# One list of token numbers in DRAM instead of two, written through two disjoint views

## The chip, the cores and the metric

The kernel runs on one core of one Trainium2 chip. The metric is the time of one execution on the device, in microseconds (us); the time of a kernel is the median of its timed runs. A profile is taken of one execution more. Five engines work side by side, each with its own queue of instructions: TensorE (PE, with its weight loads as PEld), VectorE (DVE), ScalarE (ACT), GpSimd (POOL) and SyncE (SP). They wait for each other, and for DMA transfers, through semaphores. A transfer whose rows are chosen by a list of indices (an indirect DMA) is issued from POOL's queue here, all others from SP's.

## What is computed

Three stages follow each other on 4608 tokens of width 512: chunked attention (chunks of 64), a dense layer with squared ReLU (512 to 2048 to 512), and a layer of 8 experts of which each token takes one, chosen by the largest logit.

```python
# x: [4608, 512], the output of attention
h = x @ w_in; r = np.maximum(h, 0.0); x = (s * (r * r) + b) @ w_out
logits = x @ w_gate + modality_bias[modality_id]
e_idx = np.argmax(logits, axis=1)
gate_w = softmax(logits)[arange(N), e_idx]
for e in range(E):
    mask = e_idx == e
    h = np.maximum(x[mask] @ w1[e], 0.0)
    out[mask] = gate_w[mask, None] * (h @ w2[e])
```

## The kernel before, in words

**Blocks.** The tokens are cut into 18 blocks of 256, two tiles of 128 each. For each block the dense layer runs as 16 steps f: `m_l1(j, f)` makes 128 of the 2048 hidden columns (L413), squares them on ACT and splits them into a high and a low part; the low part, gl, is a subtraction on POOL (L428). `m_l2` (L486) uses gh and gl two steps later. Attention of the next block and the routing of the block before run between these steps. The order of the instructions on every engine is the order of the program: the whole kernel is traced under a manual schedule.

**Routing.** For block j the kernel finds the expert of each token, the rank of the token among all tokens of that expert so far (`g_rank`, L635 and L636, matmuls against a triangle), and from both the place `e * 4608 + rank` (`g_dest`). `g_scatter(j)` (L658) then writes the numbers of the tokens to their places in a list in DRAM, one indirect DMA for each of the two tiles (L661). There are two lists, `ids[0]` for the first tile of every block and `ids[1]` for the second. Both are filled with 2^19 at the start (L1231); a token's number is written as number - 2^19. The sum of the two lists at a place is thus the token's number where one of the tiles wrote it, and 2^20 where none did. The rows of the tokens, scaled, go to `ys` in DRAM.

**Units.** The expert layer runs over units of 128 places in the list. `u_ids(u, idx)` (L808) gathers the 128 numbers of a unit, from both lists into two columns; `u_gather(u)` adds the columns on POOL (L816) and gathers the 128 rows of `ys` with the sum as index into `xg` (L818), where indices past the end fetch nothing. `u_x(u)` transposes xg on PE (L952) and splits it into two halves of 16 bits; `u_l1` (L973, L977) and `u_l2` (L999) are the two matmuls; the result is scattered to the rows of `out` with the same index (L1006).

**The seam between the two.** The first four units (0 to 3, "lead") belong to the expert that has most tokens after block 15; their places are filled by then, so their numbers and rows are fetched during the last block's steps. All later units need the last block's routing: `routing()` runs g_scatter(17), then `u_tables`, which works out each unit's expert and places (`gidx`, L908), then `ids_to(1)` (the numbers of units 4 and 5), `fetch` of unit 4's rows and then the numbers of unit 6. After that each unit fetches the numbers of a unit some four further on and the rows of the one three further on. PE's order is fixed: the transposes of unit 4's rows stand ahead of the second half of unit 3's first matmul.

An access to DRAM waits for earlier accesses to the same tensor that it depends on: a number gather for the landing of the scatters into its list, a scatter for the landing of the scatter before into the same list.

Of the kernel before, what the change touches and what calls it, by code (L numbers as in the profile page):

```python
# [7 lines left out]

F32 = mybir.dt.float32
# [3 lines left out]
I32 = mybir.dt.int32  # L13
U32 = mybir.dt.uint32
AF = mybir.ActivationFunctionType
ALU = mybir.AluOpType
# [2 lines left out]
DRAM = bass.MemoryType.DRAM  # L19
EXP_MASK = 0x7F800000  # L20


HALF = 1 << 19


def pow2(n):
# [4 lines left out]
def kernel(  # L31
# [16 lines left out]
    nc = tc.nc  # L48
    P = 128
    B, H, S, HD = q.shape  # L50
    NT, DM = out.shape
    FF = w_in.shape[1]
    E, _, F2 = w1.shape
# [4 lines left out]
    NTB = TB // P  # L58
    NB = NT // TB
    NTILE = NT // P  # L60
# [14 lines left out]
    def pool(name, bufs=1, side="left", st=None):  # L75
# [5 lines left out]
    dram = ctx.enter_context(tc.tile_pool(name="dram", bufs=1, space=DRAM))  # L81
# [6 lines left out]

    ys = dram.tile([NT, ROW], F32, name="ys")

    ids = [dram.tile([E * NT + P, 1], I32, name=f"ids{t}") for t in range(NTB)]
    wgt = dram.tile([E, DM], F32, name="wgt")
    wd = [
        dram.tile([E * P, 4096 + (TAIL if i == 0 else 0)], F16, name=f"wd{i}") for i in range(4)
# [9 lines left out]
        out=tri, in_=ones, pattern=[[1, P]], compare_op=ALU.is_gt, fill=0.0,  # L104
        base=0, channel_multiplier=-1,
# [3 lines left out]
    def iota(name, shape, pattern, base=0, cm=0):  # L109
        ti = tmp.tile(shape, I32, tag="i", name=name + "_i")  # L110
        nc.gpsimd.iota(ti, pattern=pattern, base=base, channel_multiplier=cm)
        tf = const.tile(shape, F32, name=name)
        nc.vector.tensor_copy(tf, ti)
        return tf
# [1 line left out]
    rev8 = iota("rev8", [P, NTB, E], [[0, NTB], [-1, E]], base=E)  # L116
    ebase = iota("ebase", [P, NTB, E], [[0, NTB], [NT, E]])
    tokid = const.tile([P, NTILE], I32, name="tokid")
    nc.gpsimd.iota(tokid, pattern=[[P, NTILE]], base=-HALF, channel_multiplier=1)
    eidx = iota("eidx", [P, E], [[1, E]])  # L120
    slot = iota("slot", [P, NRP], [[0, NRP]], cm=1)
    uidx = iota("uidx", [P, NRP], [[1, NRP]])
# [35 lines left out]
    def small(n, shape, dt=F32, bufs=None):  # L158
        return sm.tile(shape, dt, tag=n, name=n, **({"bufs": bufs} if bufs else {}))
# [498 lines left out]
    def g_scatter(j):  # L658
        di = rank.pop(j)
        for t in range(NTB):  # L660
            nc.gpsimd.indirect_dma_start(  # L661
                out=ids[t], out_offset=bass.IndirectOffsetOnAxis(ap=di[:, t, :], axis=0),
                in_=tokid[:, j * NTB + t:j * NTB + t + 1], in_offset=None,
            )

# [102 lines left out]
    uid = {}  # L768
# [34 lines left out]
        nc.sync.dma_start(out=dst, in_=wd[i][bass.ds(e * P, P), cols], **kw)  # L803

    def u_ids(u, idx):
        two = uid[u] = small("uid2", [P, NTB], I32, 6)
        for t in range(NTB):
            nc.gpsimd.indirect_dma_start(  # L808
                out=two[:, t:t + 1], out_offset=None, in_=ids[t],
                in_offset=bass.IndirectOffsetOnAxis(ap=idx, axis=0),  # L810
            )

    def u_gather(u):
        two = uid[u]
        uid[u] = small("uid", [P, 1], I32, 10)
        nc.gpsimd.tensor_tensor(out=uid[u], in0=two[:, 0:1], in1=two[:, 1:2], op=ALU.add)  # L816
        n = KNOWN_ROWS if u < NE else NT
        nc.gpsimd.indirect_dma_start(  # L818
            out=xg_t[u % 3], out_offset=None, in_=ys[:n],
            in_offset=bass.IndirectOffsetOnAxis(ap=uid[u], axis=0),  # L820
            bounds_check=n - 1, oob_is_err=False,
        )
# [284 lines left out]
    with tc.manual_schedule(engines=ENG):  # L1107
# [2 lines left out]
        nc.vector.memset(one_f, 1.0)  # L1110
        nc.vector.tensor_copy(one, one_f)
        none = su.tile([P, E * NTILE + 1], I32, tag="misc", name="none")
        nc.vector.memset(none, HALF)
        a_load(0)
        a_load(1)
        c_load(0)
# [66 lines left out]
        for s in range(2, NF + LEAD + LAG):  # L1183
# [43 lines left out]
                a_load(4)  # L1227
            if s == 7:
                nc.sync.dma_start(out=wg4, in_=w_gate.rearrange("(c p) e -> p c e", p=P))
                for t in range(NTB):  # L1230
                    nc.sync.dma_start(out=ids[t].rearrange("(p n) a -> p (n a)", p=P), in_=none)  # L1231
            if s == 8:
                v_load(4)
            if s == 9:
# [19 lines left out]
            if s == 17:  # L1254
# [6 lines left out]
                    out=wgb, in_=wgt.rearrange("e d -> (e d)").partition_broadcast(P)  # L1261
# [9 lines left out]
    with tc.manual_schedule(engines=ENG):  # L1271
# [46 lines left out]
        for f in range(NF):  # L1318
# [30 lines left out]
            if f == SCATTER:  # L1349
                g_scatter(j - 1)  # L1350
            if f in (4, 6, 8, 10):
                n = f // 2 - 2
                u_ids(n, early["gi"][:, n:n + 1])
            if f in (7, 9, 11):
                u_gather((f - 7) // 2)
# [131 lines left out]
```

## Time and profile before

| | us |
|---|---|
| timed runs, three | 1437.5, 1443.72, 1445.77 |
| their median | 1443.72 |
| the profiled execution's own time | 1438.02 |
| its span in the trace | 1436.3 |
| PE busy in the span | 1394.2 (97%) |
| DVE, ACT, POOL busy | 1070.7, 724.1, 435.7 |

The span goes from the first to the last instruction that the trace shows; 1.7 us lie around it. Busy times are of one engine each and overlap. [...]

### The profile page before, as it was taken

How to read it: one execution, taken by the hardware profiler on the slowest of the kernel's cores; microseconds unless marked ns; L12 is line 12 of the kernel's file. 1: busy time of each engine (PE TensorE's matmuls, PEld its weight loads, DVE VectorE, ACT ScalarE, POOL GpSimd, SP SyncE). 2: the span in 40 equal slices, each digit the busy share in tenths (PEclk: the TensorE clock that was granted, in tenths of full speed). 3: DMA queues.
4: the chain of work that ended last, by engine and by line, in shares of the span. 5: the costliest groups of instructions: out<-in, count | busy, mean ns of one | idle time of the engine just before them, and what ended most of it. 6: DMA issues, size and time to landing. Idle time of an engine off the chain costs nothing. (4 is left out here: it accounts for less than half of the span.)

```text
span 1436.3 us, 32039 instructions
## 1 busy us (share of the span) xinstructions
PE 1394.2 (97%) x11853; PEld 1151.0 (80%) x11853; DVE 1070.7 (75%) x2643; ACT 724.1 (50%) x1658; POOL 435.7 (30%) x515
## 2 busy tenths in 40 slices
PE   6899999999999999999999999998999999999995
PEld 5787888888888888888888888886767766776773
DVE  6987688877977977887697787767676676677662
ACT  4975555656565656655656565543233323333331
POOL 0000232332323333223323223463533433443320
PEclk9999999999999999999999999999999999999998
DMA  8673355555446443534534443461211231535340
GB/s 202 182 200 111 82 131 157 130 149 159 131 126 176 117 131 111 157 98 125 148 111 118 126 133 111 105 215 31 64 53 45 105 106 39 194 122 182 129 151 18
DMA packets 183886, 178.86 MB, mean 125 GB/s; under 512 B 131108, under 2 KB 139556, under 8 KB 179504
## 3 DMA queue, kind: packets, MB, share of 16 engines
q1 hardware_dynamic: 173392, 157.82, 37.7%
q0 software_dynamic: 10336, 18.97, 4.3%
q8 instruction: 95, 1.56, 0.5%
q14 instruction: 63, 0.52, 0.1%
HBM read 263.85 MB, written 54.14 MB: 221 GB/s over the span
## 5 line engine op out<-in xcount | busy, mean ns | idle before, releaser
L428 POOL TENSOR_TENSOR gl<-g,gh 128x256 fp32r<-128x256 f32 x256 | 221.6, 867 | 680.7 <-ACT gh L426 395.8
L413 PE MATMUL ph<-x,wi 128*128 128x256 f32 x2592 | 348.2, 285 | 5.0 <-ACT wi L232 3.8
L413 PEld LDWEIGHTS ph<-x,wi 128*128 128x128 f32 x2592 | 331.1, 190 | 20.2 <-ACT wi L232 4.4
L486 PE MATMUL py<-wo,gh 128*128 128x512 f32 x864 | 271.5, 395 | 0.2 <-DVE wo L166 0.2
L985 ACT ACTIVATE hr<-hr,scu 128x128 f32<-128x128 f32 x328 | 114.3, 396 | 282.0 <-DVE hr L166 262.4
L544 DVE CUSTOM_DVE_ANT_0 dump<-rows,wgb 128x512 bf16<-128x512 f32 x256 | 198.5, 775 | 5.0
L999 PEld LDWEIGHTS <-hh 128*128 128x128 f16 x984 | 95.0, 98 | 108.5 <-issue 2.2
L486 PE MATMUL py<-wo,gl 128*128 128x512 f32 x432 | 170.4, 395 | 0.0
L423 ACT ACTIVATE g<-ph 128x256 f32<-128x256 f32 x256 | 97.4, 380 | 136.1 <-PE ph L413 129.1
L486 PEld LDWEIGHTS py<-wo,gh 128*128 128x128 f32 x864 | 148.1, 188 | 21.8 <-DVE wo L166 0.5
L722 DVE SCALAR_TENSOR_TENSOR hl<-raw,wup,hl 128x512 f16<-128x512 f32 x128 | 111.1, 908 | 31.5 <-ACT hl L715 31.5
L973 PE MATMUL pu<-xhl,wa 128*128 128x256 f16 x736 | 127.9, 275 | 0.0
L977 PE MATMUL pu<-xhl,wa 128*128 128x128 f16 x736 | 125.4, 220 | 0.0
L999 PE MATMUL po<-wa,hh 128*128 128x512 f16 x552 | 124.6, 383 | 0.0
L715 ACT ACTIVATE hl<-raw,wup 128x512 f16<-128x512 f32 x128 | 85.5, 715 | 71.6 <-DVE wup L163 49.3
L413 PE MATMUL ph<-x,wj 128*128 128x256 f32 x864 | 116.7, 285 | 1.8 <-DVE wj L166 1.8
L981 DVE COPY hr<-pu 128x256 f32<-128x256 f32 x164 | 68.9, 420 | 61.5 <-PE pu L977 46.6
L1006 POOL DMA_INDIRECT out_dram<-o,uid x41 | 42.8, 1044 | 235.7 <-ACT o L1005 217.0
L413 PEld LDWEIGHTS ph<-x,wj 128*128 128x128 f32 x864 | 108.7, 189 | 6.3 <-DVE wj L166 2.0
L424 ACT ACTIVATE g<-g 128x256 f32<-128x256 f32 x256 | 107.5, 420 | 8.1
L426 ACT ACTIVATE gh<-g 128x256 fp32r<-128x256 f32 x256 | 107.4, 419 | 8.1
L973 PE MATMUL pu<-xhl,wb 128*128 128x256 f16 x576 | 98.9, 273 | 0.0
(216 smaller groups left out, 2271.9 us busy)
## 6 DMA issues: line engine op xcount, KB each, us to landing
wa<-wd SPq DMA_DIRECT2D x64, 1024.0 KB
wb<-wd SPq DMA_DIRECT2D x60, 1024.0 KB
raw<-in_moe_w_dram SPq DMA_DIRECT2D x64, 512.0 KB
wd<-hl SPq DMA_DIRECT2D x128, 256.0 KB
wb<-wd SPq DMA_DIRECT2D x20, 1030.5 KB
wa<-wd SPq DMA_DIRECT2D x20, 1030.5 KB
ys<-rows SPq DMA_DIRECT2D x18, 513.0 KB
vs<-in_v_dram SPq DMA_DIRECT2D x136, 64.0 KB
```

What stands on the lines that cost most here:

```text
L413: nc.tensor.matmul(ps, lhsT=wi_f(a, f)[:, kc], rhs=xt[j][b][:, kc, :], start=(n == 0), stop=(n == 3 * KC - 1),)
L423: nc.scalar.activation(out=g, in_=ps, func=AF.Relu)
L424: nc.scalar.activation(out=g, in_=g, func=AF.Square)
L426: nc.scalar.activation(out=hi, in_=g, func=AF.Copy)
L428: nc.gpsimd.tensor_tensor(out=lo, in0=g, in1=hi.bitcast(F32), op=ALU.subtract)
L486: nc.tensor.matmul(yps[j][t], lhsT=g[a][:, t * P:(t + 1) * P], rhs=wo_f(b, f), start=(f == 0 and n == 0), stop=(f == NF - 1 and n == 2),)
L544: nc.vector.tensor_tensor_reduce(out=dump, in0=ysb[j][:, t, :DM], in1=wgb[:, e * DM:(e + 1) * DM], scale=1.0, scalar=0.0, op0=ALU.mult, op ...
L722: nc.vector.scalar_tensor_tensor(out=hl[:, 1], in0=raw[:, a], scalar=sc, in1=hl[:, 0], op0=ALU.mult, op1=ALU.subtract)
L973: nc.tensor.matmul(ps[:, f], lhsT=w[:, kc, 0, cols], rhs=hl[:, :, kc, :], start=(kc == 0), stop=False,)
L977: nc.tensor.matmul(ps[:, f, 0], lhsT=w[:, kc, 1, cols], rhs=hl[:, 0, kc, :], start=False, stop=(kc == KC - 1),)
L985: nc.scalar.activation(out=r[:, f, :], in_=r[:, f, :], func=AF.Relu, scale=scu[:, c:c + 1])
L999: nc.tensor.matmul(ps, lhsT=hh[:, a, c, :], rhs=w[:, c % 4, b, :], start=(n == 0), stop=(n == 3 * NC2 - 1),)
```

## The change

The two lists become one. Both tiles of a block still scatter with one indirect DMA each, but into the same list, each through a view of its own; the views are declared disjoint, so that an access through the one isn't ordered against one through the other, while a read of the whole list is ordered behind both. Token numbers are written as they are, and an empty place holds 2^20. A unit gathers its numbers once, straight into the tile that serves as index; the add is gone. The initial fill is one store.

```diff
@@ -4,6 +4,7 @@
 import concourse.tile as tile
 from concourse import mybir
 from concourse._compat import with_exitstack
+from concourse.ap import dram_disjoint_views
 from concourse.masks import make_identity
 
 F32 = mybir.dt.float32
@@ -19,8 +20,7 @@
 DRAM = bass.MemoryType.DRAM
 EXP_MASK = 0x7F800000
 
-
-HALF = 1 << 19
+NONE = 1 << 20
 
 
 def pow2(n):
@@ -88,7 +88,8 @@
 
     ys = dram.tile([NT, ROW], F32, name="ys")
 
-    ids = [dram.tile([E * NT + P, 1], I32, name=f"ids{t}") for t in range(NTB)]
+    ids = dram.tile([E * NT + P, 1], I32, name="ids")
+    ids_v = dram_disjoint_views(ids, NTB)
     wgt = dram.tile([E, DM], F32, name="wgt")
     wd = [
         dram.tile([E * P, 4096 + (TAIL if i == 0 else 0)], F16, name=f"wd{i}") for i in range(4)
@@ -116,7 +117,7 @@
     rev8 = iota("rev8", [P, NTB, E], [[0, NTB], [-1, E]], base=E)
     ebase = iota("ebase", [P, NTB, E], [[0, NTB], [NT, E]])
     tokid = const.tile([P, NTILE], I32, name="tokid")
-    nc.gpsimd.iota(tokid, pattern=[[P, NTILE]], base=-HALF, channel_multiplier=1)
+    nc.gpsimd.iota(tokid, pattern=[[P, NTILE]], base=0, channel_multiplier=1)
     eidx = iota("eidx", [P, E], [[1, E]])
     slot = iota("slot", [P, NRP], [[0, NRP]], cm=1)
     uidx = iota("uidx", [P, NRP], [[1, NRP]])
@@ -659,7 +660,7 @@
         di = rank.pop(j)
         for t in range(NTB):
             nc.gpsimd.indirect_dma_start(
-                out=ids[t], out_offset=bass.IndirectOffsetOnAxis(ap=di[:, t, :], axis=0),
+                out=ids_v[t], out_offset=bass.IndirectOffsetOnAxis(ap=di[:, t, :], axis=0),
                 in_=tokid[:, j * NTB + t:j * NTB + t + 1], in_offset=None,
             )
 
@@ -803,17 +804,13 @@
         nc.sync.dma_start(out=dst, in_=wd[i][bass.ds(e * P, P), cols], **kw)
 
     def u_ids(u, idx):
-        two = uid[u] = small("uid2", [P, NTB], I32, 6)
-        for t in range(NTB):
-            nc.gpsimd.indirect_dma_start(
-                out=two[:, t:t + 1], out_offset=None, in_=ids[t],
-                in_offset=bass.IndirectOffsetOnAxis(ap=idx, axis=0),
-            )
+        uid[u] = small("uid", [P, 1], I32, 10)
+        nc.gpsimd.indirect_dma_start(
+            out=uid[u], out_offset=None, in_=ids,
+            in_offset=bass.IndirectOffsetOnAxis(ap=idx, axis=0),
+        )
 
     def u_gather(u):
-        two = uid[u]
-        uid[u] = small("uid", [P, 1], I32, 10)
-        nc.gpsimd.tensor_tensor(out=uid[u], in0=two[:, 0:1], in1=two[:, 1:2], op=ALU.add)
         n = KNOWN_ROWS if u < NE else NT
         nc.gpsimd.indirect_dma_start(
             out=xg_t[u % 3], out_offset=None, in_=ys[:n],
@@ -1110,7 +1107,7 @@
         nc.vector.memset(one_f, 1.0)
         nc.vector.tensor_copy(one, one_f)
         none = su.tile([P, E * NTILE + 1], I32, tag="misc", name="none")
-        nc.vector.memset(none, HALF)
+        nc.vector.memset(none, NONE)
         a_load(0)
         a_load(1)
         c_load(0)
@@ -1227,8 +1224,7 @@
                 a_load(4)
             if s == 7:
                 nc.sync.dma_start(out=wg4, in_=w_gate.rearrange("(c p) e -> p c e", p=P))
-                for t in range(NTB):
-                    nc.sync.dma_start(out=ids[t].rearrange("(p n) a -> p (n a)", p=P), in_=none)
+                nc.sync.dma_start(out=ids.rearrange("(p n) a -> p (n a)", p=P), in_=none)
             if s == 8:
                 v_load(4)
             if s == 9:
```

## Rows read from the trace of the kernel before

**Rows 1.** The page, busy time, share of the span and instructions of each engine

```profile
PE 1394.2 (97%) x11853; PEld 1151.0 (80%) x11853; DVE 1070.7 (75%) x2643; ACT 724.1 (50%) x1658; POOL 435.7 (30%) x515
```

**Rows 2.** Busy time by stage; columns: stretch, length, each engine's busy time, clock, DMA share

```profile
160.00:926.00 766.00, 763.61 (x6615) 675.76 (x6614) 606.94 (x1581) 455.23 (x1043) 240.36 (x274) 1.00 0.47 129
...
985.00:1010.00 25.00, 22.55 (x181) 15.96 (x179) 19.78 (x57) 6.50 (x18) 14.05 (x15) 0.93 0.20 63
1010.00:1385.00 375.00, 375.00 (x3158) 264.14 (x3157) 256.74 (x580) 119.20 (x309) 143.74 (x171) 1.00 0.32 108
```

**Rows 3.** Waits of PE from 900 us on: who waited for whom, total, times, longest

```profile
PE px L952 <- DMA xg<-ys,uid: 2.5, 1, 2.5
PE prk L636 <- DVE oh L166: 2.3, 1, 2.3
```

**Rows 4.** Timeline of POOL and DVE, 984 to 1001 us: start, length, engine, line, what

```profile
984.64 1.01 POOL L661 DMA_INDIRECT ids<-tokid,di  x1 [19.58 <-DVE cnt L861]
...
985.96 0.97 POOL L661 DMA_INDIRECT ids<-tokid,di  x1 [0.30 <-issue]
...
990.51 0.20 DVE L908 SCALAR_TENSOR_TENSOR gidx<-row,slot 128x40 int32<-128x40 f32 x1
...
994.04 1.10 POOL L808 DMA_INDIRECT uid<-ids,gidx  x1 [7.11 <-DMA ids<-tokid,di]
...
995.45 1.07 POOL L808 DMA_INDIRECT uid<-ids,gidx  x1 [0.30 <-issue]
...
998.25 0.95 POOL L808 DMA_INDIRECT uid<-ids,gidx  x1 [0.30 <-issue]
...
999.22 0.20 POOL L816 TENSOR_TENSOR uid<-uid 128x1 int32<-128x1 int32 x1
...
999.69 1.11 POOL L818 DMA_INDIRECT xg<-ys,uid  x1 [0.27 <-issue]
```

**Rows 5.** Timeline of PE, 1003 to 1016 us

```profile
1003.19 0.66 PE L952 MATMUL px<-ident,xg 128*128 128x128 f32 x4 [2.45 <-DMA xg<-ys,uid]
1003.68 0.27 PE L973 MATMUL pu<-xhl,wa 128*128 128x256 f16 x1
...
1007.98 5.34 PE L999 MATMUL po<-wa,hh 128*128 128x512 f16 x24
...
1013.16 0.27 PE L973 MATMUL pu<-xhl,wa 128*128 128x256 f16 x1
...
1015.80 0.39 PE L952 MATMUL px<-ident,xg 128*128 128x128 f32 x2
```

**Rows 6.** Half microseconds without and with DMA packets, columns as in rows 2

```profile
988.00:988.50 0.50, 0.50 (x9) 0.47 (x7) 0.47 (x2) 0.00 (x0) 0.00 (x0) 1.00 0.00 0
...
996.00:996.50 0.50, 0.50 (x4) 0.26 (x3) 0.47 (x2) 0.00 (x0) 0.50 (x1) 1.00 0.04 1
```

**Rows 7.** Clock after two idles of PE, columns as in rows 2, and the earlier one's wait

```profile
1005.00:1007.00 2.00, 2.00 (x15) 1.53 (x13) 1.90 (x5) 0.00 (x0) 1.32 (x1) 0.50 0.34 131
...
116.00:118.00 2.00, 2.00 (x20) 2.00 (x19) 1.93 (x5) 1.97 (x4) 0.00 (x0) 1.00 0.05 12
...
PE ph L413 <- DVE wj L166: 1.8, 1, 1.8
```

**Rows 8.** POOL's groups of instructions with count, busy, mean ns; and one wait, 1010 to 1385 us

```profile
L808 POOL DMA_INDIRECT uid<-ids,gidx x74 | 71.6, 968 | 29.4 <-issue 21.3 <-DMA ids<-tokid,di 7.1 <-DVE hr L166 0.9
...
L816 POOL TENSOR_TENSOR uid<-uid 128x1 int32<-128x1 int32 x41 | 9.4, 229 | 0.9
...
POOL out_dram L1006 <- ACT o L1005: 179.4, 32, 5.8
```

**Rows 9.** Timeline of POOL and PE behind an earlier block's scatters, 864 to 873 us

```profile
864.20 0.98 POOL L661 DMA_INDIRECT ids<-tokid,di  x1 [0.15 <-issue]
...
866.98 0.73 POOL L428 TENSOR_TENSOR gl<-g,gh 128x256 fp32r<-128x256 f32 x1 [0.51 <-issue]
...
872.18 0.40 PE L486 MATMUL py<-wo,gl 128*128 128x512 f32 x1
```

## The prediction

> **What bounds the kernel now.** I read the page first. TensorE (PE) is busy for 1394.2 of the 1436.3 us of the span, GpSimd (POOL) for 435.7 [rows 1]. A change that takes work off POOL can therefore only pay where PE waits for POOL, so the next view is the busy time by stage. From 160 to 926 us PE is busy 763.61 of 766.00 us, and from 1010 to 1385 us, where the experts' units run, 375.00 of 375.00; only the 25 us from 985 to 1010 stand out in the part that the change touches, with 22.55 busy and a granted clock of 0.93 [rows 2]. The waits of PE say what it lacked there: from 900 us to the end the list has three, and one of them ends in something that the change touches: the transposes of line 952 waited 2.5 us for the rows that unit 4 gathers (xg). The 2.3 us of the ranking matmul are DVE's and stay; the third is 0.2 us [rows 3].
>
> The timeline of POOL and DVE shows what makes unit 4's rows late. Unit 4 is the first whose tokens are known only after the last block was routed. POOL issues the last block's two scatters at 984.64 and 985.96. The indices for the number gathers are ready when DVE ends gidx at 990.51 + 0.20 = 990.71, but the first number gather starts at 994.04, after 7.11 us of idle that the scatter ended. Then come four number gathers (two lists, units 4 and 5), the last from 998.25 to 999.20, the add at 999.22 and the row gather at 999.69, which takes 1.11 us [rows 4]. PE resumes at 1003.19, that is 2.39 us after the issue of the row gather ended [rows 4, 5]. Everything in that chain is in one file on POOL, and PE has nothing else to do.
>
> **The change part by part, on the path.** (1) After the change the first number gather reads the one list, so it waits for both tiles' scatters instead of the first's alone. Call the delay d. It isn't above 995.45 - 994.04 = 1.41 us, because the gather from the second list started at 995.45 behind an idle of just 0.30 us on issue and so found its scatter landed; it isn't below 0 unless one list makes the scatters land sooner, for which no row speaks. The two scatters are issued 985.96 - 984.64 = 1.32 us apart [rows 4]; I take half of that, d = 0.7, since the second one had the same time or less to land and nothing shows when in those 1.41 us it did. (2) One gather for unit 4 (1.10 us) and one for unit 5 (1.07 us, with 0.30 us of issue before it) remain of the four [rows 4]: the first ends at 994.04 + 0.7 + 1.10 = 995.84, the second at 995.84 + 0.30 + 1.07 = 997.21, and POOL is free for the row gather near 997.5. (3) The add is gone, and with it the cover: the row gather itself now waits for unit 4's numbers to land. The nearest row for that is the DMA share: the gather whose issue ended at 995.14 shows its packets between 996.0 and 996.5, so within 1.4 us of the end of its issue [rows 4, 6]. That lands the numbers near 995.84 + 1.4 = 997.2; with 0.5 us to notice it, as an estimate between the 0.30 of an issue that waits for nothing and a little more, the row gather starts at 997.7 instead of 999.69: 2.0 us sooner. The bounds: at best d = 0 and the row gather goes as soon as POOL is free, 994.04 + 1.10 + 0.30 + 1.07 + 0.30 = 996.8, which is 2.9 us sooner and closes the whole 2.45 us; at worst d = 1.41 and the numbers need the 2.7 us from 996.52 (end of unit 4's second number gather) to 999.22 (the add that didn't have to wait): 994.04 + 1.41 + 1.10 + 2.7 + 0.3 = 999.55, 0.1 us sooner. Behind the waiting row gather stand unit 6's numbers and the output scatter of a finished unit; nothing on PE waits for either within 10 us. So PE's wait falls from 2.45 to about 0.45 us: **2.0 us**, between 0.1 and 2.45.
>
> (4) The wait costs twice. After it the granted clock is at the lower of its two levels, 0.50 from 1005 to 1007 [rows 7], and the 32 matmuls of the half unit that begins at 1003.68 last until 1007.98, 4.30 us, while the same half unit takes from 1013.16 to 1015.80, 2.64 us, at the full clock [rows 5]: 1.66 us. An idle of 1.8 us, near 115 us, left the clock at 1.00 [rows 7]. If 0.45 us remain (or anything under 1.8, that is, if the row gather comes 0.65 us sooner or more), I expect no fall: another **1.66 us**.
>
> What is late next? The rows of unit 5 are needed at 1015.80 [rows 5], their chain moves forward with unit 4's, and from 1010 on PE has no wait at all, so the 3.7 us stay gained; the end of the kernel hangs on PE's order and moves with it.
>
> [...] From 988.0 on, through eleven half microseconds, the trace has no DMA packet under way (the first of them in [rows 6]), so the scatters' are through; yet the number gather goes only at 994.04 [rows 4]. [...]
>
> **The change off the path.** The 41 adds go, at 0.23 us, and as many number gathers, at 0.97 us [rows 8]: 40 + 9 us of POOL, 61 with the 0.30 us of issue ahead of each gather. In the unit loop they lie in the time in which POOL waits for ScalarE's output tile (179.4 us over 32 waits between 1010 and 1385 us [rows 8]) while PE is full [rows 2]: worth 0. There the numbers are fetched one unit ahead of the row gather, so the missing add exposes no landing. Were that cover gone, each unit would pay some 2 us. Between 926 and 964 four of the removed gathers and the adds stand among the gl subtractions of the last block; PE's waits name none of those [rows 3]: 0. The initial fill is one store on SP's queue instead of two, long before the first scatter and beside a busy PE: 0. The constant that marks an empty slot and the base of the token numbers change no instruction's length. The scatters of the 17 earlier blocks keep their count; each of the two views has its own previous scatter one block earlier, as each list had: 0.
>
> **The sum.** 2.0 + 1.66 = 3.7 us (0.1 to 4.1) against the profiled execution's 1438.02 us: 1434.3. The three timed runs are 1437.5, 1443.72 and 1445.77; their median is 5.7 us above the profiled execution, more than the whole gain. I go by the mean of the four, 1441.3, and take 3.7 off: **1437.6, rounded to 1438**.
>
> **Rivals.** *The scatters land later when they share a list.* Six microseconds without a packet pass from 988.0 to the release of the first gather [rows 4, 6]; the 4-byte writes of one tile land slowly, and now the second tile's go to places right behind the first's. Should the second have to queue behind the first, d is 6 rather than 0.7: the row gather would start at 994.04 + 6 + 1.10 + 1.4 + 0.5 = 1003.0, 3.3 us later than now, with PE's wait at 5.8 us, the fall of the clock kept and perhaps doubled: 3.3 to 5.0 us slower than the base, 1444.6 to 1446.3. It loses against the old kernel from d = 2.7 on. Against it: the second list's gather had no wait at 995.45, so that two scatters in flight together don't hold each other up much. [...] Chance 0.12.
>
> *The new wait takes the old one's place.* With d near 1.4 and numbers that need over 2 us, the row gather starts no sooner than 999.1, the wait stays above 1.8 us and the clock falls as before: 0.1 to 0.6 us gained, 1441. For it: the bound of 2.7 us isn't excluded. Against it: packets 1.4 us after an issue. Chance 0.15.
>
> *The change doesn't do what it says: the two views are still ordered.* Then each block's second scatter waits until the first has landed, 994.04 - 985.65 = 8.4 us after its issue by [rows 4], and on POOL the next block's gl stands behind it. In the block at 864.20, the second scatter would go at 865.18 + 8.4 = 873.6 and the gl that ran at 866.98 would end near 875.3, 3.1 us after PE takes it at 872.18 [rows 9]. From 5.2 us of hold on it costs; with the clock 3.1 to 4.8 us in each of some 16 blocks, 50 to 77 us, and 7 more at the end: about 1495 to 1522, slower. Against it: the diff gives each tile a view of its own, and the old lists were kept apart in the same way. Chance 0.03.
>
> **Chances and range.** Forecast (gain 2.7 to 4.1): 0.70, at 1438. The three rivals: 0.15, 0.12, 0.03. A change of 0.5% is 7.2 us, about what a measurement of this kernel can tell from no change; no case but the last reaches it by itself, so that mainly the 8 us between timed runs could carry the forecast over it (0.11), and the first rival the other way. Faster 0.11, within 0.5% 0.82, slower 0.07. The range: the lowest timed run less 4.1 is 1433.4; the highest as it stands is 1445.8. **1433 to 1446.**
>
> **What would show it.** In the trace after: 41 number gathers and no add; the first late one near 994.7; the row gather of unit 4 near 3.7 us behind it, not 5.65; PE's wait at the xg transposes under 0.7 us; a granted clock of 1.00 from 1003 to 1009; the stage from 1010 on unchanged in length. Wrong if the first late number gather starts after 995.5 (the first rival), if it starts in time but the row gather follows by over 4.5 us (the second), or if idle time stands between the two scatters of a block (the third).

## The result

The changed kernel takes 1420.97 us (median of 4 runs, 1419.3 to 1422.85) against 1442.28 us (median of 4, 1437.5 to 1445.77) for the kernel before: a ratio of 0.9855, interval 0.9822 to 0.9887. It is 1.5% faster, where 0.3% was forecast and 1433 to 1446 us was the range. The profiled execution took 1421.37 us, its span is 1419.7 us against 1436.3: **16.6 us shorter**. These 16.6 us are what is taken apart here. The medians differ by 21.3 us (16 to 26 by the interval); what the 4.7 more are made of, or whether they are noise, no trace shows.

The page of the kernel after, busy time by engine (compare [rows 1]):

```profile
PE 1383.7 (97%) x11853; PEld 1144.4 (81%) x11853; DVE 1068.3 (75%) x2643; ACT 721.7 (51%) x1658; POOL 390.7 (28%) x433
```

POOL lost 82 instructions, the 41 adds and 41 gathers. What the forecast doesn't contain is in the first entry: TensorE executes the same 11853 matmuls and is busy for 10.5 us less. The same matmuls must have become faster somewhere.

To find where, I followed both kernels' matmul streams, which are the same instruction by instruction, and noted how far the kernel after is ahead at three marks:

| mark | before | after | gained in this part |
|---|---|---|---|
| ranking matmul of the last block, behind its 2.35 us wait | 979.75 | 973.08 | 6.7 |
| end of the last matmul | 1421.46 | 1411.20 | 3.6 |
| end of the span | 1436.3 | 1419.7 | 6.3 |

So three parts, of which the forecast has one, the middle one.

**The dense stretch.** The scatters frame it. Their group of instructions in the kernel before and in the one after; columns: duration in ns (least, median, longest), start of the first and of the last in us:

```profile
L661 POOL DMA_INDIRECT ids<-tokid,di x36: 972/979/1127, 165.0 to 986.0; - x36
```

```profile
L662 POOL DMA_INDIRECT ids<-tokid,di x36: 967/987/1136, 166.0 to 979.3; - x36
```

From the first scatter to the last it is 821.0 us before and 813.3 after: 7.7 us less. (The start of the kernel, ahead of the first scatter, was 1.0 us longer, so that 6.7 are left at the first mark.) PE is full in both (763.61 of 766.00 in [rows 2]), so no wait went. The matmuls themselves got shorter; the groups of PE by shape from 160 to 950 us, first before, then after (busy, mean ns | idle ahead):

```profile
L413 PE MATMUL ph<-x,wi 128*128 128x256 f32 x2244 | 299.6, 283 | 0.3 <-ACT g L423 0.3
```

```profile
L414 PE MATMUL ph<-x,wi 128*128 128x256 f32 x2246 | 294.4, 280 | 0.1
```

The mean of 283 against 280 ns hides two paces. From the start of one of these matmuls to the start of the next, where both are of this line, the trace has steps of about 113 and about 118 ns. I call the share of steps over 115 ns the **long share**: it is 0.90 before and 0.25 after. Summed over the stretch, the steps between two matmuls of this line take 330.0 us before and 322.6 after: 7.4 of the 7.7 us. The long share is the mark for the experiments below. Why a change of POOL's list should move it was the first question.

**The seam.** Waits of PE from 900 us on, after (compare [rows 3]):

```profile
PE prk L637 <- DVE oh L167: 2.4, 1, 2.4
PE px L949 <- DMA xg<-ys,uid: 1.2, 1, 1.2
PE pu L970 <- DVE xhl L167: 0.8, 1, 0.8
PE prk L636 <- DVE xf L167: 0.2, 1, 0.2
```

Timeline of POOL after, 970 to 1000 us, with two lines of DVE's, against [rows 4], and PE's behind it, against [rows 5]:

```profile
977.97 1.01 POOL L662 DMA_INDIRECT ids<-tokid,di  x1 [19.78 <-DVE cnt L858]
979.29 0.99 POOL L662 DMA_INDIRECT ids<-tokid,di  x1 [0.30 <-issue]
983.84 0.20 DVE L905 SCALAR_TENSOR_TENSOR gidx<-row,slot 128x40 int32<-128x40 f32 x1
986.00 0.42 DVE L167 TENSOR_TENSOR hr<-pu,hr 128x256 f32<-128x256 f32 x1
987.21 0.98 POOL L808 DMA_INDIRECT uid<-ids,gidx  x1 [6.94 <-DVE hr L167]
988.50 0.96 POOL L808 DMA_INDIRECT uid<-ids,gidx  x1 [0.31 <-issue]
990.66 1.01 POOL L815 DMA_INDIRECT xg<-ys,uid  x1 [1.20 <-issue]
```

```profile
994.58 0.66 PE L949 MATMUL px<-ident,xg 128*128 128x128 f32 x4 [1.24 <-DMA xg<-ys,uid]
995.07 0.27 PE L970 MATMUL pu<-xhl,wa 128*128 128x256 f16 x1
...
997.71 5.34 PE L996 MATMUL po<-wa,hh 128*128 128x512 f16 x24
```

The view puts the 6.94 us down to DVE's `hr`, but the first number gather doesn't read that tile, and its indices (`gidx`) were ready at 984.04. The trace's records name what it waited for: the semaphores of the two scatters, whose last updates came at 985.58 and 986.36; the gather starts 0.85 us after the later one. In 16 of the 17 other kernels with one list it does so 0.76 to 0.91 us after it; the trace of the 17th lacks most of these updates. So the wait is for both scatters to land.

Two number gathers instead of four, then 1.20 us in which the row gather waits for numbers to land (the view says issue; in the records the wait for unit 4's numbers ends at 989.94), and the row gather. It starts 12.69 us behind the block's first scatter instead of 15.05. PE goes on 994.58 - 973.08 = 21.50 us behind the ranking matmul instead of 1003.19 - 979.75 = 23.44. The half unit behind it takes 997.71 - 995.07 = 2.64 us instead of 4.30. The granted clock tells why: the share of full speed that the trace's clock records give for PE, 0.50 or 1.00 in every record of both kernels, with a mean where a stretch holds some of both. Stretches of the kernel before and of the kernel after (columns as in [rows 2]), each first behind the ranking matmul, then at the half unit:

```profile
980.50:984.00 3.50, 3.50 (x10) 1.18 (x8) 2.67 (x11) 2.73 (x7) 0.00 (x0) 0.51 0.01 2
1004.50:1008.00 3.50, 3.50 (x26) 2.80 (x24) 3.20 (x8) 0.00 (x0) 2.53 (x4) 0.52 0.40 115
```

```profile
973.50:977.50 4.00, 4.00 (x20) 1.85 (x20) 3.14 (x13) 2.72 (x7) 0.00 (x0) 1.00 0.01 2
994.00:996.00 2.00, 1.42 (x15) 1.35 (x16) 1.01 (x3) 0.69 (x2) 1.28 (x2) 1.00 0.35 131
```

Both falls to 0.5 are gone, the one behind the untouched 2.35 us wait too.

**The end.** The last piece of the chain of work that ended last, and the span, before and after:

```profile
1423.28 0.68 POOL out_dram L1006
```

```profile
core 0: 1436.3 us, clock 0.990
```

```profile
1412.66 0.69 POOL out_dram L1003
```

```profile
core 0: 1419.7 us, clock 0.993
```

The chain ends with the issue of the last output scatter; behind it the span goes on for 1436.3 - 1423.96 = 12.3 us before and 1419.7 - 1413.35 = 6.3 us after. The views count no instruction there as busy. The trace's records have POOL's last instruction in it, a drain (`DRAIN`) of 7.74 us before and 4.39 us after, and ahead of it an instruction on the semaphores of POOL's DMAs (`INC_SWDGE_SEM`, 2.07 and 1.27 us) at the end of the branch over the last, optional units. I call it the join; both paths, the one through the branch and the one past it, meet there.

### The profile page after: what moved, and what is told of

Its sections match the earlier page's. It is cut to its first block, busy times and chain, and to the rows that moved or that the text cites. A ratio compares the mean times of both kernels' runs of the same rounds, so it can differ in the third digit from the quotient of the medians.

```text
span 1419.7 us, 31880 instructions
## 1 busy us (share of the span) xinstructions
PE 1383.7 (97%) x11853; PEld 1144.4 (81%) x11853; DVE 1068.3 (75%) x2643; ACT 721.7 (51%) x1658; POOL 390.7 (28%) x433
## 5 line engine op out<-in xcount | busy, mean ns | idle before, releaser
L429 POOL TENSOR_TENSOR gl<-g,gh 128x256 fp32r<-128x256 f32 x256 | 225.8, 884 | 674.5 <-ACT gh L427 404.3
L414 PE MATMUL ph<-x,wi 128*128 128x256 f32 x2592 | 343.9, 283 | 3.9 <-ACT wi L233 3.1
L414 PEld LDWEIGHTS ph<-x,wi 128*128 128x128 f32 x2592 | 327.3, 190 | 18.8 <-ACT wi L233 3.8
```

Source lines behind the costliest of these rows:

```text
L414: nc.tensor.matmul(ps, lhsT=wi_f(a, f)[:, kc], rhs=xt[j][b][:, kc, :], start=(n == 0), stop=(n == 3 * KC - 1),)
L429: nc.gpsimd.tensor_tensor(out=lo, in0=g, in1=hi.bitcast(F32), op=ALU.subtract)
```

## The experiments

All 18 are compared with the kernel before on the same chip (its median there is given, since it differs by chip: 1434.0 to 1442.6). A time without a range is one run. "Stretch" is from the first scatter to the last, as above; before 821.0, after 813.3. Each trace is of one execution.

**What made the dense matmuls faster?** The change removed the tile `uid2`: 6 buffers of 32 bytes in each partition, 192 bytes from the pool of small tiles that lies ahead of those of the dense layer. Everything allocated behind that pool moved down by 192 bytes. Theory: the place of a tile sets the pace. Rival: POOL's or the DMAs' lighter work does. One kernel gives the change its 192 bytes back, one leaves the kernel before as it is, but for allocating `uid2` in a pool opened later.

```diff
 (after)
     def u_ids(u, idx):
+        if u == 0:
+            small("pad", [P, 48], I32, 1)
         uid[u] = small("uid", [P, 1], I32, 10)
 (before)
-        two = uid[u] = small("uid2", [P, NTB], I32, 6)
+        two = uid[u] = late[0].tile([P, NTB], I32, tag="uid2", name="uid2", bufs=6)
```

> The changed kernel with an unused tile of 192 bytes a partition in the pool of small tiles, so that all tiles of the pools opened behind it (g, gh, gl, rows, wgb, raw, hl, xg, the unit's weights) lie at the addresses of the kernel before. Between the first tile's scatter of block 0 and that of block 16 the kernel before took 961.20 - 165.00 = 796.2 us and the changed one 954.52 - 166.0 = 788.5. Theory A, placement in SBUF: the stretch goes back to 796, the mean of the L414 matmuls from 280 to 283 ns, the time from 1421 to about 1428.5. Theory B, the removed fill store (which moves every later transfer of SP's queue to another of its semaphores): nothing moves, 788.5 and 1421. Theory C, chance between executions: either, without relation to the edit. The end (span end less last matmul, 14.8 before and 8.5 after) stays 8.5 by A and B.

> The kernel before, two lists and all its instructions, with only its two-column tile of numbers (uid2, 192 bytes a partition) moved to a pool that opens in the last block: the tiles of the dense layer and the routing lie at the changed kernel's addresses, those of the units at the old ones. Theory A, placement: the stretch of blocks 0 to 16 goes from 796.2 to 788.5 us and the time from 1442 to about 1434.5. Theory B, the removed fill store: 796 and 1442. The seam (PE's wait of 2.45 us at the transposes) and the end (14.8 us) stay by both.

The scatters and the dense matmuls (views as above) of the change with the unused 192 bytes:

```profile
L662 POOL DMA_INDIRECT ids<-tokid,di x36: 967/987/1137, 166.2 to 988.3; - x36
```

```profile
L414 PE MATMUL ph<-x,wi 128*128 128x256 f32 x2248 | 300.1, 283 | 0.2 <-ACT g L424 0.2
```

And of the kernel before with its tile moved:

```profile
L661 POOL DMA_INDIRECT ids<-tokid,di x36: 969/977/1123, 164.7 to 977.6; - x36
```

```profile
L413 PE MATMUL ph<-x,wi 128*128 128x256 f32 x2244 | 293.9, 280 | 0.0
```

The stretch changes sides: 822.1 us (long share 0.90) for the changed kernel with an unused tile, 812.9 (0.25) for the old kernel with two lists, adds and all. The times follow: 1431.98 us (1431.22 to 1432.62) against 1441.62, ratio 0.9938 (0.9921 to 0.9954), and 1433.64 us (1428.44 to 1437.82) against 1441.62, 0.9949 (0.9929 to 0.997). So the dense stretch's gain has nothing to do with token lists; the edit's content, seam and end, is worth 0.6%, and the place of some tile about half a per cent.

**Which tile, and which places?** With the 192 bytes inserted further and further on, all behind the insertion stands at its old place and all ahead at its new one: ahead of `g`, between `g` and `gh`, between `gh` and `gl`, behind `gl`. The edit is one line with an unused tile, here the one ahead of `gh`; the others are the same line elsewhere.

```diff
+        if (j, f) == (2, 0):
+            g_p.tile([P, 48], I32, name="pad", bufs=1)
         hi = g_p.tile([P, TB], F32R, tag="gh", name="gh")
```

> The changed kernel with 192 unused bytes a partition between wgb and the pool of g, gh and gl, so that g, gh, gl, raw and hl lie at the addresses of the kernel before, and the late weights of the second matmul (wt), rows, dump and wgb at the changed kernel's. If what counts is where the weight loads of L487 read gh and gl (or another tile of these two pools): the stretch of blocks 0 to 16 is 796 to 797 us, as with all of them moved (797.3). If it is wt, rows or wgb: 788.5.

> The changed kernel with 192 unused bytes between g and gh inside their pool: gh and gl, which PE loads as weights in L487, lie at the old addresses, g (which only ACT and POOL read) at the new ones. With g, gh and gl at the old addresses the stretch of blocks 0 to 16 was 796.1 us, with raw and hl alone there 786.7. If the weight loads count: 796. If ACT's and POOL's reads and writes of g count: 787 to 788.5.

> The same bytes between gh and gl: gl alone (and raw and hl, shown not to count) at the old addresses. gl is a third of the weight loads of L487, gh two thirds, and the last load ahead of the next L414 matmuls is one of gl. If the state in which a line of matmuls begins decides, that last load counts and the stretch is 796; if each load counts for itself, about a third of the way, 790 to 791; if only gh counts, 787 to 788.5.

> The same 192 bytes one pool later: only raw and hl, which PE never reads, lie at the old addresses; g, gh and gl at the changed kernel's. If the weight loads from gh and gl count: 788.5 us for the stretch. If it is a clash with the transfers into raw and out of hl: 796 to 797.

Then the size of the shift, as in the first kernel but with 64, 128 and 256 bytes:

> The changed kernel with 64 unused bytes in the pool of small tiles: all the later tiles move by 64, gh from 81408 (a multiple of 512) to 81472. The kernel before had it at 81600, 192 off. If only a multiple of 128 or more is good, the stretch is 796; if 64 is enough, it is 788.5, but then the 192 of the kernel before, also a multiple of 64, would have been good too, which it wasn't: I expect 796 or, if the cost grows with the offset, something between.

> The changed kernel with all later left-side tiles, gh and gl among them, moved by 128: gh at 81536. Known: at 81408 the stretch of blocks 0 to 16 is 787 to 788.5 us, at 81472 it was 794.2, at 81600 796. If what is good repeats every 128 bytes: 788. If it repeats only every 256 or 512: 794 to 796.

> The changed kernel with all later left-side tiles moved by 256: gh at 81664. If what is good repeats every 128 or 256 bytes: 788; if only every 512: 794 to 796.

Then the other operands of the dense matmuls, the weights `wo`, `wi`, `wj`, which lie at the other end of the memory: moved by 32, 64 and 480 bytes, by 32 together with `gh` and `gl`, and by 256 (`wo` by 224). The edit is an unused tile in a pool of its own ahead of them.

```diff
+    pad_r, _ = pool("pad_r", side="right", st=ctx)
+    pad_r.tile([P, 120], I32, name="pad_r")
     wo_p, wo_st = pool("wo", side="right")
```

> The changed kernel with wi, wj and wo 32 bytes lower, gh and gl where they were. Moving wi, wj and wo by 480 had brought the slow pace back (794.4). Theory distance: this changes the distance by 32 too, 794 to 796. Theory address: gh and gl still begin on a multiple of 512; if their address alone counts 788, if wi has good and bad addresses of its own either.

> The changed kernel with wi, wj and wo 64 bytes lower (114592 for wi; 114656 was good, 114624 and 114176 were bad), gh and gl at their good place. Both bad moves changed the place of wi by an odd multiple of 32, and the moving operand of L414, x, hasn't moved: if the two have to lie a multiple of 64 apart, 64 lower is good again, 787 to 789.5 for the stretch of blocks 0 to 16. If wi is good only where it was, 794 or more.

> The changed kernel with 480 unused bytes at the far end of the right side, which puts the resident weights of both dense matmuls (wi, wj, wo) on multiples of 512, where they were 480 off. gh and gl are on such multiples already; a quarter of the L414 matmuls, the first few behind each L487, are still at the slower pace (118 against 113 ns). If it is any weight load off such a multiple that puts PE into the slower pace, the rest goes too: about 2350 matmuls x 0.25 x 4.5 ns = 2.6 us off the stretch, 785 to 786, and 1418.5 in time. If the offset of these tiles doesn't matter: 1421.

> The changed kernel with gh and gl 32 bytes lower (one buffer of the index tiles less) and the resident weights wi, wj, wo 32 bytes lower as well: their distance is that of the changed kernel, their addresses aren't. Theory distance (the load of one weight tile and the read of the other clash by their distance): 788. Theory address (gh and gl must begin on a multiple of at least 128): 794 to 796.

> The changed kernel with wo 224 bytes lower, on a multiple of 256, and wi and wj 256 bytes lower, a multiple of 64 from where they were; gh and gl at their good place. With wo on a multiple of 512 (right512) the mean step of the L487 matmuls was 231.9 ns instead of 234.7, while wi was off and cost more than that gave. If 256 is enough for wo and 64 for wi: L414 stays at 117.8 ns of mean step, L487 goes to 232, the stretch to about 784 and the time to 1417, 4 us below the changed kernel. If one of the two isn't enough: 788 or 792 to 794.

What they gave ("gh at" is the byte offset of `gh` in each partition by the program's allocation; after is at 81408, a multiple of 256, before at 81600):

| edit to the kernel after | gh at | us (before) | stretch | long share |
|---|---|---|---|---|
| none | 81408 | 1420.97 (1442.28) | 813.3 | 0.25 |
| 192 bytes ahead of g, gh, gl | 81600 | 1429.89 (1434.0) | 820.9 | 0.91 |
| 192 ahead of gh, gl | 81600 | 1431.51 (1436.39) | 821.2 | 0.91 |
| 192 ahead of gl alone | 81408 | 1424.84 (1436.39) | 814.9 | 0.53 |
| 192 behind gl | 81408 | 1417.5 (1434.0) | 811.4 | 0.23 |
| 64 ahead of all | 81472 | 1426.54 (1434.0) | 818.9 | 0.92 |
| 128 ahead of all | 81536 | 1428.2 (1442.62) | 816.9 | 0.40 |
| 256 ahead of all | 81664 | 1423.27 (1442.62) | 814.8 | 0.26 |
| weights by 32 | 81408 | 1433.69 (1442.62) | 822.7 | 0.95 |
| weights by 64 | 81408 | 1435.48 (1436.28) | 824.9 | 0.98 |
| weights by 480 | 81408 | 1428.78 (1436.39) | 819.1 | 0.92 |
| weights by 32, gh and gl by 32 | 81376 | 1432.96 (1442.62) | 824.2 | 0.95 |
| wi, wj by 256, wo by 224 | 81408 | 1421.1 (1436.28) | 812.0 | 0.20 |

For the weights by 480 the ratio is 0.9952 (0.9936 to 0.9969), for the last row 0.9894 (0.9876 to 0.9912); these two have four runs each. What follows: (a) the tiles that count are `gh` and `gl`, the ones that PE loads as stationary operand (the one that a weight load puts in place) in line 487. With `g` at its new place and these two at the old one, the long step is back whole; `gl` alone brings back part of it, and what lies behind them nothing. (b) In these five places the pace repeats with 256 bytes: shifts of 0 and 256 have the short step (long share 0.25 and 0.26), 64 and 192 the long one (0.92 and 0.90), and 128 lies in between (0.40). (c) At the other end there are good and bad places too: a shift of `wi` and `wj` by 256 and of `wo` by 224 keeps the pace while 32, 64 and 480 lose it. For 64 and 480 the short pace had been expected. The weights alone aren't shown to be the cause there, since the attention tiles that open behind them on that side move with them. A theory that only the distance between the two groups counts fell with the row that moves both by 32. (d) Moving the weights found nothing faster than the change as it is: the last row's interval overlaps that of the change, 0.9855 (0.9822 to 0.9887), and its 1421.1 us are not the 1417 hoped for. What in the memory makes the place matter, and which of the tiles at the other end does, stays open.

**Do the gathers or the add make the seam?** Every number gather is issued twice, the second time into a tile that nobody reads; the add stays away.

```diff
+        nc.gpsimd.indirect_dma_start(
+            out=late[0].tile([P, 1], I32, tag="again", name="again", bufs=6), out_offset=None,
+            in_=ids, in_offset=bass.IndirectOffsetOnAxis(ap=idx, axis=0),
+        )
```

> The changed kernel with every number gather issued twice, the second into a tile that nobody reads (in a late pool, so that the dense layer's placement stays): POOL issues 200 indirect transfers again instead of 159, without the add. My reading of the seam: three more issues stand ahead of unit 4's row gather (1.3 us each, of which about one is covered by the numbers' landing), so it starts 1.0 to 1.5 us later than the 12.7 us behind the first scatter that it has now, and PE's wait grows from 1.2 to some 2.2 to 2.7 us. The end: if the drain of POOL at the end of the program grows with the number of indirect transfers, span end less last matmul goes from 8.5 back to about 14.8 us and the time to about 1429; if not, it stays 8.5 and the time is 1422 to 1424. The dense stretch stays 788.5.

Its timeline of POOL from 970 us:

```profile
980.75 1.01 POOL L662 DMA_INDIRECT ids<-tokid,di  x1 [19.81 <-DVE cnt L863]
...
990.98 0.99 POOL L809 DMA_INDIRECT uid<-ids,gidx  x1 [7.92 <-DVE hh L991]
992.27 1.02 POOL L813 DMA_INDIRECT again<-ids,gidx  x1 [0.31 <-issue]
993.60 0.94 POOL L809 DMA_INDIRECT uid<-ids,gidx  x1 [0.30 <-issue]
994.85 0.94 POOL L813 DMA_INDIRECT again<-ids,gidx  x1 [0.30 <-issue]
996.10 1.01 POOL L820 DMA_INDIRECT xg<-ys,uid  x1 [0.30 <-issue]
```

1439.58 us against 1441.62. The dense stretch keeps most of its gain (815.7 us, long share 0.27), but the row gather is back at 15.35 us behind the first scatter, PE waits 2.73 us for it, the drain is back at 7.74 us, and from the ranking matmul to the last one it takes 446.5 us against 438.1. Counted from the first number gather, the row gather starts after 996.10 - 990.98 = 5.12 us, after 3.45 in the change and after 5.65 before: the two gathers more are worth 1.7 us there, the add some 0.5. So it is mainly the gathers' issue that was on the path, and their number that the end pays for. The time is 10 us above the 1429 expected. The 446.5 are 4.8 us more than before's 441.7; 2.9 of them are six waits of the second matmul (line 1001), put down to issue, which no other run has at that size. I have no cause for those.

**Is the disjointness what the change needs?** Both tiles scatter through the whole list.

```diff
-    ids_v = dram_disjoint_views(ids, NTB)
+    ids_v = [ids] * NTB
```

> The changed kernel without the disjoint views: both tiles scatter through the list itself, so that the second scatter of a block waits for the first to land. This is the third rival of the prediction as a kernel. By its working each of some 16 blocks loses 3.1 to 4.8 us and the seam some 7 more: 1478 to 1505. If the low parts (gl) that queue behind on POOL have more slack than I read, it is less: the seam's 7 us alone give 1428.

Its waits of PE from 160 us on, and what POOL's scatters were released by:

```profile
PE py L487 <- POOL gl L429: 52.8, 15, 9.4
PE px L949 <- DMA xg<-ys,uid: 8.7, 1, 8.7
```

```profile
  DMA ids<-tokid,di: 112.8, 15
```

1506.73 us against 1441.62. From block 0's first scatter to block 16's it takes 862.4 us instead of 788.5: 74 us, where the prediction's third rival said 50 to 77. A second scatter waits 112.8 / 15 = 7.5 us for the first to land, `gl` stands behind it on POOL, and PE behind `gl`. One list is a gain only because its two halves aren't ordered.

**What is the end made of?** One kernel adds a single number gather (160 indirect DMAs instead of 159), which also moves the turn of the DMA semaphores by one; the other puts two more into the optional units, which aren't executed.

```diff
 (one more)
+        if u == 0:
 (in the branch)
+        if u >= NU - 2:
 (both)
+            nc.gpsimd.indirect_dma_start(
+                out=late[0].tile([P, 1], I32, ...), out_offset=None, in_=ids,
+                in_offset=bass.IndirectOffsetOnAxis(ap=idx, axis=0),
+            )
```

> The changed kernel with one number gather of unit 0 issued twice: 160 indirect transfers instead of 159. With 159 the drain of POOL at the end took 4.39 us and span end less last matmul was 8.5; with 200 it took 7.74 and 14.8 to 15.5, and the last transfer was on the eighth of the eight semaphores that these transfers take in turn (200 is a multiple of 8). Theory count: the drain grows by 82 ns per transfer, 4.47 us here, and the end stays 8.5. Theory turn (the end is long when the last transfer falls on the eighth semaphore, so that POOL waits for its landing first): 160 is a multiple of 8 too, POOL waits for the landing, some 2 us more: 10.5 with a drain of 4.5, or 14.8 if the drain hangs on the turn as well. The time is 1421 by the first, 1423 to 1427 by the second.

> The changed kernel with each number gather of the two units in the skipped branch at the end issued twice: the run still issues 159 indirect transfers, but the branch that isn't taken holds eight of them, as in the kernel before, instead of six, so that the join behind it touches all eight semaphores and has to wait for the landing of the last output scatter. Expected: the drain stays 4.39 us, the join goes from 1.27 to 2.07 us and starts some 2.2 us later, span end less last matmul 8.5 + 3.0 = 11.5. If the join has nothing to do with it: 8.5.

The end of the chain and the span, with one gather more, then with eight indirect DMAs in the skipped branch instead of six:

```profile
1409.28 0.69 POOL out_dram L1009
```

```profile
core 0: 1416.3 us, clock 0.996
```

```profile
1410.68 0.72 POOL out_dram L1009
```

```profile
core 0: 1419.6 us, clock 0.992
```

With one more, 6.3 us remain behind the last issue, as after, and the drain is 4.475 instead of 4.393 us: 82 ns for one DMA, and (7.742 - 4.393) / 41 = 82 ns again for the 41 between the two kernels. From 159 to 200 the drain's length goes with the number of indirect DMAs executed; it isn't in proportion to it (159 times 82 ns would be 13 us), so fewer than 159 may cost by another rule. The turn of the semaphores plays no part in it. With eight in the branch, 8.2 us remain, 1.9 more, at the same drain of 4.39 us: the join behind the branch starts that much later. In the kernel before it likewise held eight. The records show why: ahead of the join POOL waits for every DMA semaphore that the skipped branch could have used, eight of them before (111 to 118) and six in the change. With eight in the branch, the one of the last output scatter is among them: its last update comes at 1412.96 and POOL goes on at 1412.99; before, at 1425.54 and 1425.56. In the change, with six, there is no wait for that semaphore. So of the 6.3 us, 3.35 are the drain, about 1.9 the join's wait for the last landing, and 0.8 the join's own length, 2.07 against 1.27; that last also stayed at 1.25 with eight in the branch, and was 2.07 in every run with 200 executed DMAs, so that it goes with the count and not with the branch. I had expected it with the branch.

## Why the prediction was wrong

**The sum on the path held.** (1) The delay d, taken as 0.7 between 0 and 1.41: in the profile after, the first number gather comes 9.24 us behind the first scatter, before 9.40, so d = -0.16. But in the 16 other kernels with the two views it comes 9.73 to 11.04 us behind, and in the kernel before with its tile moved 8.89: d is there 0.3 to 1.6 against the 9.40 and 0.8 to 2.2 against the 8.89, so 0.7 is on the low side and 1.41 no bound. That "nothing shows" when the second scatter landed is not so: in the records of the trace of before its semaphore has its last update at 993.86, the first scatter's at 993.27, 0.6 us apart. (2), (3): the row gather goes 3.45 us behind the first number gather, where 3.7 was asked for, and 2.36 us sooner against the scatter, where 2.0 was forecast; it starts 2.5 us after the end of their issue, 0.6 more than the 1.9 taken and inside the bound of 3.0 (2.7 and 0.3 of issue). (4) The clock stayed at 1.00 behind a wait of 1.24 us, as forecast for anything under 1.8, and gave 1.66 us. Together 3.6 us against 3.7, a closer match than the sum deserves: it is that of the execution with the lowest d of all.

One number in it was wrong: PE's wait fell to 1.24 us, not to 0.45. The rows came 1.9 us sooner, and PE itself got there 0.7 us sooner, because the clock didn't fall behind the ranking matmul either. That alone put PE 1.7 us ahead, of which a new wait for DVE's `xhl` (0.8 us, line 970) took a part. I had not foreseen it, and nothing ties it to the change: with the same 2.35 us wait it fell in eight of the 15 kernels that differ from the change in placement or by one or two gathers. The profiled execution is thus one of the best, by luck: from the ranking matmul to the last one the kernel before takes 441.7 us and its variant with the tile moved 443.4, the change 438.1, and those 15 take 438.1 to 440.6, 439.1 in the middle, which is a gain of 2.6 against before. Three patterns make these up. In eight the clock fell behind the ranking matmul, PE came later and waited 1.69 us at most for the rows, with no second fall. In five it didn't, PE came early, waited 1.92 to 2.04 us, and the clock fell there (440.4 to 440.6): the rival "the new wait takes the old one's place", in its fall of the clock at least. In two, and in the change's own profile, it fell at neither. Before, and in the two other kernels that issue four gathers ahead of the rows, it fell at both.

**The step that failed is the part off the path.** It costed each removed thing at nothing, and for the instructions that was right: 1010 to 1385 us is full in both kernels, and 45 us less of POOL (435.7 to 390.7) bought nothing there. But it listed instructions only. *The removed tile* is also an edit, and moved all tiles behind it: 7.7 us, twice the whole forecast. And "the end of the kernel hangs on PE's order and moves with it" overlooked that 14.8 us of the span lie behind the last matmul, 12.3 of them behind the last piece of the chain; 41 DMAs less and two DMAs less in a branch that isn't even executed took 6.3 of them. The rows to ask were there: the chain's last piece ends 12.3 us ahead of the span's end. With these two terms the sum would have been 3.7 + 7.7 + 6.3 = 17.7 and the time 1441.3 - 17.7 = 1423.6; the base of 1441.3 was right (1442.28 measured). The first term couldn't have been sized from the trace of before, the second could, in part.

**The rivals.** "The scatters land later when they share a list" needed d = 2.7 to decide; no run shows more than 2.2. The second scatter's last semaphore update comes 6.7 and 6.9 us after the end of its issue in the kernels with two lists, 6.1 to 7.8 us after it in those with one, so that no queue of 6 us shows. In the change the second one's issue ended at 980.28 and its semaphore has its last update at 986.36, 6.1 us later and 2.3 us behind the indices, which were ready at 984.04: the landing set the start of the first number gather. "Views still ordered" was priced rightly, 74 us measured in the blocks for 50 to 77, and didn't occur.

## What to carry to other kernels

A tile that an edit removes or resizes moves all tiles behind it, and where PE is the bound its operands' place can be worth more than the edit, here 7.7 us against 3.6 at the seam: read the pace of the untouched matmuls first, and put an unused tile of the old size back to tell the edit from its layout. Look at what stands between the last matmul and the end of the span (14.8 us before, 8.5 after), and count indirect DMAs for it, those of skipped branches too. A wait is worth more than its length where the clock falls behind it (here 1.66 us on top of 2.45), but whether it falls can change between kernels that differ in an unused tile or one or two gathers (behind the ranking matmul it did in eight of 15), so such a term wants a range.

## What the runs showed of the hardware

- The 128x256 matmul of line 414 goes every 113 or every 118 ns, by the place of the operands of another, interleaved matmul: with `gh` at 81408 or 81664 bytes, `gl` moved with it and the weights unmoved 0.22 to 0.29 of the steps are long (the kernels of the other experiments included), with the two 64 or 192 bytes above 81408 it is 0.90 to 0.92; over the dense stretch that is 7.7 us for 192 bytes. With the tiles at the other end moved by 32, 64 or 480 bytes it is 0.92 to 0.98, by 256 (`wo` by 224) 0.20.
- At the end of the program POOL's drain takes 82 ns more for each further indirect DMA that was executed, between 159 and 200 of them (4.393 us for 159, 4.475 for 160, 7.742 for 200).
- Two more DMAs in a branch that isn't taken made the end 1.9 us later: POOL waits behind it for the semaphores that the branch would have used, and the last output scatter's was then among them (updated at 1412.96, POOL went on at 1412.99).
- The clock's fall behind an idle of PE isn't fixed: behind the same 2.35 us it was there in eight of 15 kernels that differ little, and not in the other seven; behind the wait for unit 4's rows it stayed at full speed after 1.1, 1.24 and 1.8 us (192 bytes behind `gl`, the change, one gather more), and fell after 1.92, 2.04 and 2.45 us.
- A scatter of 128 numbers of 4 bytes is seen as landed late: the gather that waits for both tiles' goes 6.9 to 8.7 us after the second issue has ended, and before, where it waited for the first tile's alone, 994.04 - 985.65 = 8.4 us after that one's. Of these, 0.8 to 0.9 lie between the semaphore's last update and the gather's start. In the trace of before no packet is under way from 988.0 to 994.5 [rows 6], and the two scatters' last updates come at 993.27 and 993.86.
